# Strassen's products for five token blocks in place of four, with a newly drawn order of steps

## The chip, the cores and the metric

The kernel runs on 1 core of one Trainium2 chip. The metric is the device time of one execution in microseconds (us), median of three runs. Engines are named as the profile names them: PE is TensorE's matmul pipe and PEld its weight loads, DVE is VectorE, ACT is ScalarE, POOL is GpSimd, SP is SyncE, which issues nearly all DMAs.

## The reference

Linear attention over 8 batches and 8 heads, followed by two large products with a gate between them. All data is float32.

```
q_s = softmax(q, axis=-1)            # q, k, v: (8, 8, 576, 64)
k_s = softmax(k, axis=2)
kv  = einsum('bhsd,bhse->bhde', k_s, v)
a   = einsum('bhsd,bhde->bhse', q_s, kv)
x   = a.transpose(0, 2, 1, 3).reshape(4608, 512)
h   = x @ w_in                       # w_in:  (512, 2048)
g   = h * cos(h)
out = g @ w_out                      # w_out: (2048, 512)
```

## The kernel before

The 4608 tokens are nine blocks of 512: block b (0 to 7) holds the first 512 tokens of batch b, block 8 the 64 tokens left over from each batch. The 2048 columns of `h` are 16 slices f of 128. A **unit** u is one block times one slice, 144 in all. Blocks 0 and 1 are done by halves (units 0 to 31 are blocks 0 and 1, slices 0 to 7, then 8 to 15), and from unit 32 each block is 16 units in a row: block 2 is units 32 to 47, block 3 is 48 to 63, block 4 is 64 to 79, block 5 starts at unit 80.

A float32 product is made from three products of split operands (high part, low part): weights `wh`, `wl` against data `xh`, `xl`, without `wl*xl`. An ordinary unit (`unit1`) multiplies 4 chunks of 128 rows of `w_in` by the 128x512 block of x: 4 x 3 = 12 matmuls of 512 columns into one PSUM bank `h` (line 1159). Then the gate runs on ACT and DVE in turn: `turns` (ACT, line 1165), `rest` (DVE, 1169), `cos` (ACT, 1175), `gate` (DVE, 1181), the high part `ghi` (ACT, 1192) and the low part `glo` (DVE, 1198). `unit2` adds the unit's share of the output into four banks `acc` (PE, line 1402, 12 matmuls), two units later.

Blocks from `SB` on go another way for the first product: two slices f, f+1 at a time, `products(u)` uses Strassen's method in Winograd's form on the 2x2 split of x (left and right half of its 512 rows, even and odd tokens): 7 products of 2 x 3 matmuls with 256 columns each (line 1274) in place of 24 matmuls of 512. Product names are T1, B11, B21, T2, T3, B22, T4. T1 and B11 go to a bank `pb`; ACT copies from `pb` into the two `h` banks (`seed`, line 1293) and into `p5` (line 1297), and DVE adds twice (lines 1300 and 1303). The gate and the second product are as before.

Two things have to be there for it:

- Sums and differences of the weights' quarters. `combine(a)` makes those of the slices 2a and 2a+1 (8 calls): 8 DVE steps (lines 1341 to 1364), two ACT casts (1360), and writes to `combined` in DRAM. From there SP loads pieces of 512 KB into the places of `w_in` slices 6 to 13 (`piece`), 28 for a block.
- Sums and differences of the quarters of x (`x_parts`, lines 876 to 907), in place of `x_lo` (line 1025). Their places are those of `w_in` slices 0 to 5.

So `w_in` itself must be out of use by then, and all calls of `combine` lie between unit 32 and the last unit before block `SB`, `2 * (SB - 2)` units apart.

While one block is multiplied, the attention of the next is computed on the same engines: `load_k`, `k_exps`, `kv_rows` and `k_steps` (the kv product on PE, line 710; its normalisation on DVE, lines 690 to 694, 734, 758), `q_steps` (softmax of q, lines 795 to 826), and `x_steps` (q transposed by 32x32 blocks on DVE, line 1047; x on PE, line 989). In units 0 to 23 the weights are also converted from the form in which they come in (`convert`: ACT lines 464 and 469, DVE `shift` 475 and `sign` 486, then the split 498 to 509).

Every step is first added to a `Plan` with its engine. The list `ORDER` of step numbers then sets the order in which all steps are issued; each engine, SP's queue among them, works through its own steps in that order and waits for semaphores where data is not there.

Of the kernel before, what the change touches and what calls it, by code (L numbers as in the profile page):

```python
# [48 lines left out]
    SB=5,  # L49
# [9 lines left out]
7 17 4 0 1 80 81 82 12 2 3 74 75 83 76 160 161 77 78 79 162 163 164 5 6 8 9 10 11 31 13 14 34 35 84 36 44 85 15 16 18  # L59
19 37 45 46 47 92 94 105 28 93 106 38 39 42 20 21 54 48 55 142 143 56 49 40 223 224 225 144 41 43 95 22 23 156 96 57  # L60
58 59 145 146 157 62 24 25 86 87 26 27 50 226 227 97 72 98 52 100 88 29 30 64 51 53 101 107 65 243 244 89 66 90 108
245 311 246 91 60 61 117 109 112 179 180 181 67 99 68 110 102 113 334 63 119 312 313 130 111 319 69 182 120 122 32 33
114 121 125 118 147 165 166 320 203 204 205 70 131 314 123 321 322 323 158 71 73 148 126 127 124 132 167 183 184 185
134 236 237 238 133 137 324 247 149 150 315 316 338 339 317 318 186 135 330 331 325 206 207 159 208 136 138 353 340
139 239 196 197 198 326 327 332 355 341 240 333 173 174 342 151 152 153 209 210 356 357 228 154 155 168 169 170 187
192 335 175 229 358 359 343 347 360 361 188 189 263 264 230 328 115 116 211 193 194 336 337 171 172 329 344 345 362
363 199 346 349 350 351 366 364 352 365 231 190 191 348 354 377 195 176 177 178 103 104 212 213 379 378 380 202 381
216 217 248 278 279 280 281 369 370 382 287 288 200 232 233 201 383 388 222 218 219 220 214 215 783 367 368 371 798
799 265 266 384 302 303 385 389 390 249 250 372 221 373 391 267 268 374 234 269 375 235 251 252 376 392 579 580 464
393 289 394 395 256 257 513 514 304 242 290 140 141 258 259 270 398 400 271 282 241 399 426 283 284 272 253 254 784  # L70
785 528 529 530 515 401 291 285 621 622 292 791 262 403 552 553 404 402 409 293 255 294 295 554 786 792 793 516 128
129 405 406 484 260 794 410 261 273 305 306 274 275 411 412 795 296 297 286 307 603 604 567 568 413 414 451 415 416
452 419 298 299 444 796 531 569 308 517 605 606 797 309 518 789 790 800 420 421 276 277 310 300 301 429 485 445 386
387 465 623 624 625 446 787 788 827 810 811 812 639 640 447 448 422 431 519 532 423 555 520 533 813 814 494 495 626
435 436 437 570 1084 1085 571 428 432 433 434 457 458 474 427 430 459 424 475 675 676 425 441 460 461 815 828 829 830
831 467 468 469 453 677 678 477 801 802 454 449 450 534 438 607 556 641 642 535 557 455 478 479 808 809 396 397 608
470 471 456 462 463 466 487 832 480 481 833 581 582 816 627 472 473 558 559 572 488 489 834 835 803 804 657 658 836
643 476 482 594 595 817 818 483 486 490 491 573 574 583 584 492 493 596 597 497 505 498 499 598 585 496 442 443 918
919 506 507 679 504 508 586 599 500 501 521 819 509 560 600 659 660 661 837 849 850 864 865 601 609 662 522 663 610
510 523 502 503 512 511 536 537 611 612 628 644 805 561 562 524 525 629 1298 1299 806 807 563 820 821 439 440 540 630  # L80
526 527 539 538 543 587 564 541 542 575 576 565 588 589 822 823 680 590 645 591 544 545 549 550 551 613 631 614 681
546 577 646 647 709 710 615 616 566 578 824 592 648 838 602 593 632 633 634 664 665 620 617 1440 1441 618 649 650 635
851 852 636 1129 666 682 683 667 841 842 619 638 637 668 651 652 1130 1131 1138 853 866 867 854 656 653 684 685 920
921 669 670 671 672 693 673 654 655 686 694 687 688 839 840 843 844 674 922 923 547 548 704 705 689 692 690 691 845
700 855 856 1139 703 706 707 708 714 715 695 696 697 724 846 698 699 701 725 726 825 711 712 713 857 868 858 860 719
720 847 702 716 717 718 727 728 407 408 869 861 870 735 736 737 738 739 848 879 880 826 859 731 732 733 881 882 1140
743 744 751 1141 1142 721 734 729 730 742 752 745 746 747 740 741 894 895 722 723 924 925 883 417 418 926 927 871 753
873 1132 872 875 884 885 759 874 750 748 749 758 896 897 932 934 935 754 755 767 756 757 876 886 1133 1134 887 760 761
762 928 929 763 898 930 931 933 947 948 888 890 775 1158 1151 1152 899 891 766 900 892 893 889 901 768 769 776 777 902
764 765 774 1145 903 904 905 770 771 772 906 936 937 1143 909 778 773 779 780 962 910 1135 1136 1137 782 1148 1149  # L90
1150 911 912 1159 1160 1146 1147 1153 1154 781 941 939 963 913 964 965 966 1155 1156 1157 942 943 938 944 945 946 949
877 878 1144 950 951 1016 1017 973 974 957 958 975 976 977 1161 1186 940 1162 1163 1164 1165 1166 981 952 953 989 1167
914 915 982 983 984 954 985 969 970 959 971 967 968 990 1175 1178 1179 1176 1177 1180 1181 972 978 1182 979 960 961
991 992 1183 997 1184 1185 993 1018 980 988 994 1724 1725 1187 1188 995 986 987 1005 998 1006 955 956 999 1000 996
1007 1001 1008 1197 1198 1019 1020 1199 1200 1201 1189 1190 1212 1213 1214 1215 1009 1021 862 863 1202 1203 1168 1169
1002 1003 1170 1022 1023 1026 1027 1028 1030 1031 1191 1192 1035 1036 1037 1004 1010 1011 1043 916 917 1044 1045 1469
1470 1471 1216 1038 1039 1034 1042 1171 1172 1204 1205 1193 1194 1195 1046 1029 1047 1196 1242 1243 1051 1206 1207
1059 1217 1218 1219 1052 1053 1040 1041 1050 1054 1055 1478 1048 1060 1061 1049 1479 1062 1480 1481 1056 1482 1067
1208 1173 1057 1032 1033 1086 1087 1174 1088 1089 1063 1058 1066 1221 1222 1209 1220 1090 1091 1024 1025 1092 1093
1068 1069 1064 1227 1228 1472 1473 1474 1065 1491 1492 1070 1071 1072 1075 1105 1074 1229 1230 1231 1076 1077 1078  # L100
1079 1098 1096 1097 1368 1369 1099 1106 1232 1233 1234 1082 1083 1107 1113 1223 1224 1108 1109 1235 1236 1237 1121
1498 1100 1101 1080 1244 1245 1475 1493 1499 1500 1073 907 908 1114 1488 1489 1490 1210 1211 1104 1246 1247 1081 1112
1238 1239 1248 1249 1250 1122 1094 1095 1494 1495 1123 1124 1125 1110 1111 1120 1115 1116 1117 1118 1485 1486 1487
1119 1251 1253 1252 1254 1257 1496 1497 1370 1371 1280 1258 1126 1259 1260 1102 1103 1302 1127 1261 1128 1267 1303
1304 1291 1262 1264 1483 1484 1476 1477 1501 1526 1281 1292 1282 1283 1293 1284 1294 1265 1268 1269 1270 1321 1502
1503 1504 1505 1225 1226 1506 1295 1515 1516 1517 1507 1271 1508 1509 1263 1322 1323 1324 1325 1266 1305 1306 1510
1272 1273 1274 1329 1307 1277 1287 1288 1289 1290 1285 1286 1330 1296 1511 1331 1332 1518 1519 1278 1279 1529 1530
1527 1528 1520 1521 1522 1337 1297 1333 1338 1339 1320 1328 1340 1275 1276 1308 1310 1311 1345 1523 1524 1341 1353
1525 1537 1538 1334 1531 1326 1335 1327 1300 1301 1346 1354 1347 1348 1355 1309 1552 1553 1240 1241 1532 1349 1356
1314 1357 1336 1344 1539 1540 1541 1361 1342 1343 1352 1533 1512 1542 1543 1544 1362 1363 1364 1365 1312 1313 1546  # L110
1315 1391 1350 1351 1534 1554 1555 1360 1392 1393 1394 1513 1535 1536 1514 1012 1013 1654 1655 1395 1366 1545 1556
1557 1358 1367 1399 1407 1316 1317 1786 1547 1558 1559 1787 1788 1359 1548 1390 1398 1795 1796 1797 1400 1408 1401
1402 1403 1415 1549 1409 1410 1411 1396 1397 1318 1319 1372 1561 1562 1373 1404 1798 1582 1583 1567 1568 1569 1570
1571 1789 1405 1790 1791 1808 1799 1809 1810 1584 1585 1560 1572 1563 1423 1374 1565 1566 1564 1375 1416 1417 1418
1419 1424 1425 1406 1414 1376 1377 1378 1379 1382 1383 1426 1431 1427 1255 1256 1811 1812 1813 1384 1386 1387 1385
1388 1389 1461 1802 1792 1573 1815 1412 1413 1420 1421 1803 1804 1574 1575 1586 1576 1577 1578 1579 1814 1805 1800
# [135 lines left out]
def linear_attention_then_cos_gated_mlp(  # L252
# [85 lines left out]
    q_rows = dr.tile([2, S, P], F32, name="q_rows")  # L338
    SB = CFG["SB"]
    NOP = 7 * NF // 2  # L340
# [583 lines left out]
    def x_steps(b, p, place, kvw, tq, tx, due_q, due_x, xr=None):  # L924
# [147 lines left out]
        us = 0.6 if whole else 0.37  # L1072
        if b >= SB:
            e = floats(b, p)
# [581 lines left out]
```

## Time and profile before

| | |
|---|---|
| median of three runs | 832.1 us (831.51 to 832.5) |
| the profiled execution | 831.63 us, of which the span from first to last instruction is 829.8 us |
| granted TensorE clock over the span | 1.000 |
| matmuls recorded | 4884: 960 on line 1159 (units 0 to 79), 1344 on line 1274 (units 80 to 143, 32 pairs x 42), 1656 on line 1402, and those of the attention |
| start of unit 80 (first matmul of line 1274) | 491.5 us after the span's start |

Of an engine's row the busy time is the union of its instructions. A matmul's end is modelled and reaches over the start of the next one, so what a matmul costs in a row of matmuls is read from the distance of their starts, or from a piece of the chain of work divided by its count.

### The profile page before, as it was taken

The numbers are of one execution on the slowest core, as the hardware profiler recorded it, in microseconds if no ns is written. First come the engines' busy times: TensorE is split into PE (matmuls) and PEld (weight loads), VectorE is DVE, ScalarE is ACT, GpSimd is POOL, SyncE is SP. The second block draws the span as 40 slices with busy tenths as digits, with TensorE's granted clock in tenths as the row PEclk, the third lists the DMA queues.
The fourth block names the chain that finished last, engine by engine and source line by source line (L and its number), as shares of the span: only waits on it lengthen the run. The fifth ranks groups of instructions, "written<-read, shape, count | busy, mean of one in ns | idle before, by whom it ended". The sixth has DMA issues, their size and how long they took to land.

```text
span 829.8 us, 13645 instructions
## 1 busy us (share of the span) xinstructions
PE 801.2 (97%) x4884; PEld 705.1 (85%) x4884; DVE 639.1 (77%) x1084; ACT 532.0 (64%) x958; POOL 41.6 (5%) x161
## 2 busy tenths in 40 slices
PE   2899999999999999999999999999999999999997
PEld 1666788788888888888888898999999999999996
DVE  7999999988768976888788878788877645664443
ACT  4999998655456557664764667677756546555441
POOL 1100100000100110002000110002000000000000
PEclk9999999999999999999999999999999999999999
DMA  8888182324635651563535886998788587665521
GB/s 252 258 221 310 55 273 69 106 70 119 181 83 138 176 161 45 150 183 100 152 107 146 219 254 220 252 268 261 208 234 246 198 287 238 224 199 189 188 106 51
DMA packets 196036, 149.28 MB, mean 180 GB/s; under 512 B 110464, under 2 KB 172416, under 8 KB 195968
## 3 DMA queue, kind: packets, MB, share of 16 engines
q1 hardware_dynamic: 195648, 147.89, 59.7%
q8 instruction: 38, 0.62, 0.3%
q10 hardware_dynamic: 320, 0.52, 0.2%
q14 instruction: 30, 0.25, 0.1%
HBM read 114.03 MB, written 34.34 MB: 179 GB/s over the span
## 4 chain that ended last, share of the span: by engine, by line
PE 78%; DVE 5%; ACT 4%; DMA 1%; issue 1%; SPq 1%; ACTq 0%
PE acc L1402 38%; PE h L1159 19%; PE h L1274 13%; PE pb L1274 5%; PE x_False L989 2%; PE kv L710 1%; DVE kt L1181 1%; DMA raw_o<-in_moe_w_out_dram 1%; DMA w_io<-combined 1%; DVE w_o L509 1%; ACT L1175 0%; DVE glo L1198 0%; DVE kt L1169 0%; ACT kt L1175 0%; ACT raw_io L464 0%
## 5 line engine op out<-in xcount | busy, mean ns | idle before, releaser
L1402 PE MATMUL acc<-w_o,ghi 128*128 128x512 f32 x552 | 164.5, 380 | 0.0
L1159 PE MATMUL h<-x,w_i 128*128 128x512 f32 x660 | 152.5, 383 | 2.2 <-DVE kt L1181 2.0
L1165 ACT ACTIVATE kt<-h 128x512 int32<-128x512 f32 x144 | 86.1, 600 | 106.6 <-PE h L1274 57.3
L1159 PEld LDWEIGHTS h<-x,w_i 128*128 128x128 f32 x660 | 123.5, 189 | 22.1 <-DVE kt L1181 4.1
L1169 DVE SCALAR_TENSOR_TENSOR kt<-kt,h 128x512 f32<-128x512 int32 x144 | 97.9, 684 | 41.9 <-ACT kt L1165 41.1
L1181 DVE TENSOR_TENSOR kt<-kt,h 128x512 f32<-128x512 f32 x138 | 93.6, 686 | 34.5 <-ACT kt L1175 32.7
L1175 ACT ACTIVATE kt<-kt 128x512 f32<-128x512 f32 x144 | 90.3, 633 | 46.0 <-DVE kt L1169 45.3
L1402 PEld LDWEIGHTS acc<-w_o,ghi 128*128 128x128 f32 x552 | 101.3, 189 | 12.8 <-DVE o L1449 0.2
L1402 PE MATMUL acc<-w_o,glo 128*128 128x512 f32 x276 | 105.0, 381 | 0.2 <-DVE glo L1198 0.2
L1402 PE MATMUL acc<-w_io,ghi 128*128 128x512 f32 x296 | 88.4, 380 | 0.0
L1192 ACT CAST ghi<-kt 128x512 fp32r<-128x512 f32 x106 | 64.5, 618 | 26.0 <-DVE kt L1181 18.1
L1198 DVE TENSOR_TENSOR glo<-kt,ghi 128x512 fp32r<-128x512 f32 x106 | 71.7, 685 | 11.0 <-ACT ghi L1192 10.6
L1402 PE MATMUL acc<-w_o,w_io 128*128 128x512 f32 x288 | 72.9, 379 | 0.0
L1159 PE MATMUL h<-x,w_io 128*128 128x512 f32 x300 | 68.0, 379 | 1.1 <-DVE kt L1181 1.1
L1159 PEld LDWEIGHTS h<-x,w_io 128*128 128x128 f32 x300 | 56.0, 189 | 9.1 <-DVE kt L1181 1.5
L1402 PEld LDWEIGHTS acc<-w_o,glo 128*128 128x128 f32 x276 | 52.2, 189 | 9.0 <-DVE glo L1198 1.8
L1402 PEld LDWEIGHTS acc<-w_io,ghi 128*128 128x128 f32 x296 | 53.8, 189 | 6.6
L1402 PEld LDWEIGHTS acc<-w_o,w_io 128*128 128x128 f32 x288 | 51.6, 190 | 5.7
L1402 PE MATMUL acc<-w_io,glo 128*128 128x512 f32 x148 | 56.1, 379 | 0.0
L1274 PE MATMUL h<-x,w_i 128*128 128x256 f32 x320 | 48.3, 275 | 0.0
L1274 PEld LDWEIGHTS h<-x,w_i 128*128 128x128 f32 x320 | 44.6, 191 | 1.7 <-ACT h L1293 0.2
L1274 PE MATMUL h<-w_i,w_i 128*128 128x256 f32 x280 | 44.6, 276 | 0.8 <-ACT h L1293 0.7
(155 smaller groups left out, 1321.4 us busy)
## 6 DMA issues: line engine op xcount, KB each, us to landing
w_i<-combined SPq DMA_DIRECT2D x70, 512.0 KB, 4.8
w_io<-combined SPq DMA_DIRECT2D x42, 512.0 KB, 5.0
out_dram<-o SPq DMA_DIRECT2D x32, 256.0 KB, 2.5
k<-in_k_dram SPq DMA_DIRECT2D x14, 512.0 KB, 4.3
q<-in_q_dram SPq DMA_DIRECT2D x28, 256.0 KB, 3.5
qb<-q_rows SPq DMA_DIRECT2D x96, 72.0 KB, 2.6
q_rows<-q SPq DMA_DIRECT2D x24, 256.0 KB, 2.5
raw_i<-in_moe_w_in_dram SPq DMA_DIRECT2D x11, 512.0 KB, 5.4
```

What stands on the lines that cost most here:

```text
L509: nc.vector.tensor_sub(split(l), dealt(c), split(h))
L710: nc.tensor.matmul(x[h * D : (h + 1) * D, odd : odd + vt.shape[1]], t[:, h, c, :], vt, start=(c == CM), stop=(c == CM - 1),)
L989: nc.tensor.matmul(t[:, 0:HALF], a, c[:, cs] if whole else woven(c[:, cs]), start=(n == 0), stop=(n == len(parts) - 1 and not again))
L1159: nc.tensor.matmul(o, a, woven(x), start=(c == 0 and n == 0), stop=(c == KC - 1 and n == 2))
L1165: nc.scalar.activation(t, T["h", u], AF.Identity, bias=0.25, scale=1.0 / TWO_PI)
L1169: nc.vector.scalar_tensor_tensor(t.bitcast(F32), t, -TWO_PI, T["h", u], op0=ALU.mult, op1=ALU.add)
L1175: nc.scalar.activation(t, t, AF.Sin, bias=0.5 * math.pi)
L1181: nc.vector.tensor_mul(o, t, T["h", u])
L1192: nc.scalar.copy(t, T["kt", u].bitcast(F32))
L1198: nc.vector.tensor_sub(t, T["kt", u].bitcast(F32), T["gh", u].bitcast(F32))
L1274: nc.tensor.matmul(dst(), w[:, cs], x.rearrange("p a i -> p i a"), start=start and j == 0 and n == 0, stop=j == 1 and n == 2, skip_group_c ...
L1402: nc.tensor.matmul(T["acc", j], a[:, js], woven(w), start=(first and n == 0), stop=(last and n == 2))
```

## The change

`SB` goes from 5 to 4: block 4 (units 64 to 79) is done by Strassen's products too. Its 192 matmuls of line 1159 go, 8 pairs of 42 on line 1274 come. The eight calls of `combine` now come every 4 units from unit 32 to 60, in place of every 6 from 32 to 74. `x_parts` runs for block 4 as well. The choice of due times `att2`/`att3` also shifts by one block with `SB`, but due times don't enter the program: the order does. `ORDER` is another list from its first numbers on (3769 steps in place of 3575). Lines behind the list stand 8 further down in the kernel of after.

```
-    SB=5,
+    SB=4,
...
 ORDER = """
-7 17 4 0 1 80 81 82 12 2 3 74 75 83 76 160 161 77 78 79 162 163 164 5 6 8 9 10 11 31 13 14 34 35 84 36 44 85 15 16 18
...
```

Three places show how the list moves instructions.

The first is DVE in unit 18 (block 0, slice 10), where the names carry the unit: `kt_18`, `h_18`, `glo_16`; `raw_io13` is the raw weight slice 13 in conversion, `kvw_2_2` and `kvt_2_2` belong to the attention of block 2, head pair 2. Before:

```order
L734 SCALAR_TENSOR_TENSOR kvt_2_2_1594<-kv_2_2_1487,r_2_2_1590,mask_83 128x128
L507 TENSOR_TENSOR w_io12_1581<-wc_io12_1571,w_io12_1581 128x512
L509 TENSOR_TENSOR w_io12_1581<-wc_io12_1571,w_io12_1581 128x512
L1198 TENSOR_TENSOR glo_16_1603<-kt_16_1534,ghi_16_1601 128x512
L1181 TENSOR_TENSOR kt_17_1576<-kt_17_1576,h_17_1509 128x512
L1169 SCALAR_TENSOR_TENSOR kt_18_1638<-kt_18_1638,h_18_1613 128x512
L758 TENSOR_TENSOR kvw_2_2_1641<-kvt_2_2_1594,kvw_2_2_1641 128x128
L475 SCALAR_TENSOR_TENSOR raw_io13_1150<-raw_io13_1150 128x1024
L1181 TENSOR_TENSOR kt_18_1638<-kt_18_1638,h_18_1613 128x512
L475 SCALAR_TENSOR_TENSOR raw_io15_1210<-raw_io15_1210 128x1024
```

The same place of the changed kernel, around the same `gate` of unit 18 (line 1189 there):

```order
L1189 TENSOR_TENSOR kt_17_1554<-kt_17_1554,h_17_1539 128x512
L1055 STREAM_TRANSPOSE qf_2_0_1604<-qb_2_0_1590 128x576
L1177 SCALAR_TENSOR_TENSOR kt_18_1620<-kt_18_1620,h_18_1606 128x512
L515 TENSOR_TENSOR w_io12_1601<-wc_io12_1563,w_io12_1601 128x512
L517 TENSOR_TENSOR w_io12_1601<-wc_io12_1563,w_io12_1601 128x512
L1189 TENSOR_TENSOR kt_18_1620<-kt_18_1620,h_18_1606 128x512
L483 SCALAR_TENSOR_TENSOR raw_io13_1059<-raw_io13_1059 128x1024
L494 SCALAR_TENSOR_TENSOR wc_io13_1639<-raw_io13_1059 128x1024
L1177 SCALAR_TENSOR_TENSOR kt_19_1675<-kt_19_1675,h_19_1649 128x512
L1206 TENSOR_TENSOR glo_17_1696<-kt_17_1554,ghi_17_1633 128x512
```

The `shift` of slice 13 now stands behind the gate, and so does that of slice 14, and six steps of block 2's kv (`kvw_2_1`, `kvt_2_2`, `kvw_2_2` and the three short ones of `r_2_2`); the transpose `qf_2_0` has come in ahead. The other DVE steps ahead of this gate are the same in both kernels.

The second is PE where the Strassen blocks begin: unit 80 before, unit 64 after (`pb_80`, `h_80`; `h_80` holds unit 80, `w_i7` is the place of a loaded piece). Before:

```order
L1274 MATMUL pb_80_5062<-x_5_0_4745,w_i6_857 128x256 x3
L1274 MATMUL pb_80_5062<-x_5_1_4931,w_i6_857 128x256 x3
L1402 MATMUL acc_64_0_4321<-w_io13_1689,ghi_77_5052 128x512 x2
L1402 MATMUL acc_64_0_4321<-w_io13_1689,glo_77_5054 128x512
L1402 MATMUL acc_64_1_4365<-w_io13_1689,ghi_77_5052 128x512 x2
L1402 MATMUL acc_64_1_4365<-w_io13_1689,glo_77_5054 128x512
L1402 MATMUL acc_64_2_4371<-w_io13_1689,ghi_77_5052 128x512 x2
L1402 MATMUL acc_64_2_4371<-w_io13_1689,glo_77_5054 128x512
L1402 MATMUL acc_64_3_4375<-w_io13_1689,ghi_77_5052 128x512 x2
L1402 MATMUL acc_64_3_4375<-w_io13_1689,glo_77_5054 128x512
L1274 MATMUL h_80_5091<-x_5_2_4806,w_i7_975 128x256 x3
L1274 MATMUL h_80_5091<-x_5_3_4988,w_i7_975 128x256 x3
```

After (line 1282 is 1274 of before):

```order
L1282 MATMUL pb_64_4247<-x_4_0_3973,w_i6_888 128x256 x3
L1282 MATMUL pb_64_4247<-x_4_1_4137,w_i6_888 128x256 x3
L1282 MATMUL h_65_4267<-w_i2_560,w_i7_1013 128x256
L1282 MATMUL h_65_4267<-w_i0_325,w_i7_1013 128x256
L1282 MATMUL h_65_4267<-w_i2_560,w_i7_1013 128x256 x2
L1282 MATMUL h_65_4267<-w_i1_521,w_i7_1013 128x256
L1282 MATMUL h_65_4267<-w_i2_560,w_i7_1013 128x256
L1282 MATMUL h_64_4284<-x_4_2_3994,w_i7_1013 128x256 x3
L1282 MATMUL h_64_4284<-x_4_3_4176,w_i7_1013 128x256 x3
L1282 MATMUL pb_66_4292<-x_4_0_3973,w_i9_1374 128x256
```

Before, 12 matmuls of unit 77's second product stand between B11 and the first product that needs a seed; after, T2 follows B11 at once.

The third is DVE at the end of block 3 (units 62 and 63, attention of block 4 in `x_4_...`, `xf_4_1`). Before:

```order
L1025 TENSOR_TENSOR x_4_3_4107<-x0_4_3_False_4072,x_4_3_4107 128x288
L1025 TENSOR_TENSOR x_4_3_4107<-x1_4_3_False_4076,x_4_3_4107 128x224
L1169 SCALAR_TENSOR_TENSOR kt_63_4102<-kt_63_4102,h_63_3972 128x512
L1356 TENSOR_TENSOR sum_5_4041<-sum_5_4041 128x256
L1364 TENSOR_TENSOR sum_5_4041<-sum_5_4041,sumhi_5_0_4119 128x512
L1181 TENSOR_TENSOR kt_62_4098<-kt_62_4098,h_62_3946 128x512
```

After:

```order
L893 TENSOR_TENSOR x_4_3_4176<-xf_4_1_4115,x_4_3_4176 128x512
L897 TENSOR_TENSOR xf_4_1_4115<-xf_4_1_4115 128x2x128
L1177 SCALAR_TENSOR_TENSOR kt_63_4112<-kt_63_4112,h_63_4041 128x512
L897 TENSOR_TENSOR xf_4_1_4115<-xf_4_1_4115 128x2x128 x3
L1189 TENSOR_TENSOR kt_62_4105<-kt_62_4105,h_62_4028 128x512
L913 TENSOR_TENSOR w_i1_521<-xf_4_1_4115,x_4_1_4137 128x2x2x128
L915 TENSOR_TENSOR w_i1_521<-xf_4_1_4115,w_i2_560 128x512
L1189 TENSOR_TENSOR kt_63_4112<-kt_63_4112,h_63_4041 128x512
```

Where two `x_lo` (line 1025) and `combine`'s sixth call (`sum_5`) stood, the steps of `x_parts` for head pairs 1 and 3 now stand between the last gates of block 3; the last call of `combine` (`sum_7`) lies some 40 rows further ahead.

One more place is told in words alone, as its rows read alike: ahead of unit 6's first product PE had the second products of units 0 to 3 before, and has those of units 0 to 2 after; ahead of the gate that this product waits for (unit 4's), DVE has three conversion steps of 512 columns fewer and one `x_lo` more. In front of unit 20's first product PE has three matmuls of a second product fewer than before.

## Rows read from the trace of the kernel before

**Rows 1.** The page: busy time by engine, and PE's busy tenths in 40 slices.

```profile
PE 801.2 (97%) x4884; PEld 705.1 (85%) x4884; DVE 639.1 (77%) x1084; ACT 532.0 (64%) x958; POOL 41.6 (5%) x161
...
PE   2899999999999999999999999999999999999997
```

**Rows 2.** By stretch: us, busy (x) of PE, PEld, DVE, ACT, POOL; clock, DMA share, GB/s.

```profile
40.00:160.00 120.00, 115.74 (x615) 88.05 (x616) 114.68 (x173) 108.63 (x173) 6.45 (x11) 1.00 0.53 169
160.00:225.70 65.70, 65.70 (x316) 57.92 (x315) 54.45 (x88) 36.53 (x66) 3.90 (x23) 1.00 0.48 130
225.70:405.60 179.90, 179.84 (x1058) 157.86 (x1057) 142.85 (x237) 109.17 (x177) 12.85 (x54) 1.00 0.47 129
405.60:491.50 85.90, 85.90 (x477) 75.53 (x477) 71.02 (x119) 53.47 (x93) 5.77 (x26) 1.00 0.64 183
491.50:658.90 167.40, 166.61 (x1184) 155.42 (x1182) 133.89 (x230) 113.02 (x222) 5.54 (x26) 1.00 0.81 237
```

**Rows 3.** Who PE waited for over the whole span: us, times, longest.

```profile
PE h L1159 <- DVE kt L1181: 3.1, 3, 1.3
PE h L1274 <- ACT h L1293: 0.7, 1, 0.7
```

**Rows 4.** The chain that ended last, from 120 to 160 us: start, us, what.

```profile
149.10 0.17 DVE r L691
...
154.51 1.46 DVE raw_io L475
155.97 0.64 DVE kt L1181
...
156.65 2.86 PE h L1159 x12
```

**Rows 5.** The same chain later: two of its pieces on PE.

```profile
165.98 5.18 PE h L1159 x24
...
495.69 1.34 PE h L1274 x12
```

**Rows 6.** Groups by line and shape, DVE: xcount, then busy us, mean ns, idle before.

```profile
L1047 DVE STREAM_TRANSPOSE qf<-qb 128x576 f32<-128x576 f32 x24 | 18.5, 771 | 2.3 <-DMA qb<-q_rows 2.3
...
L889 DVE TENSOR_TENSOR xf<-xf 128x256 f32<-128x256 f32 x32 | 13.6, 425 | 0.5
...
L475 DVE SCALAR_TENSOR_TENSOR raw_io<-raw_io 128x1024 int32<-128x1024 int32 x5 | 7.5, 1528 | 0.0
...
L734 DVE SCALAR_TENSOR_TENSOR kvt<-kv,r,mask 128x128 f32<-128x128 f32 x24 | 8.4, 350 | 0.6
...
L1341 DVE TENSOR_TENSOR sum<-w_i 128x512 f32<-128x512 f32 x11 | 7.5, 703 | 0.0
...
L1025 DVE TENSOR_TENSOR x<-x_False,x 128x288 fp32r<-128x288 f32 x16 | 7.2, 452 | 3.2 <-ACT x L1003 3.2
L758 DVE TENSOR_TENSOR kvw<-kvt,kvw 128x128 fp32r<-128x128 f32 x24 | 6.9, 286 | 2.0 <-ACT kvw L754 2.0
```

**Rows 7.** Groups by line and shape, ACT.

```profile
L1293 ACT COPY h<-pb 128x256 f32<-128x256 f32 x64 | 22.8, 362 | 14.5 <-DVE kt L1181 12.2 <-PE pb L1274 1.7
```

**Rows 8.** PE in order of time at the wait on line 1293: start, us, what, idle before.

```profile
515.00 0.94 PE L1274 MATMUL h<-w_i,w_i 128*128 128x256 f32 x6 [0.73 <-ACT h L1293]
```

**Rows 9.** By stretches of 20 us, columns as in rows 2.

```profile
100.00:120.00 20.00, 18.41 (x83) 15.09 (x82) 19.10 (x29) 19.31 (x28) 1.75 (x2) 1.00 0.66 202
120.00:140.00 20.00, 19.25 (x119) 16.11 (x119) 19.31 (x27) 19.43 (x25) 0.00 (x0) 1.00 0.29 102
140.00:160.00 20.00, 18.90 (x94) 15.29 (x91) 18.40 (x27) 13.47 (x23) 0.31 (x1) 1.00 0.26 93
160.00:180.00 20.00, 20.00 (x94) 17.53 (x93) 18.37 (x28) 11.90 (x20) 0.00 (x0) 1.00 0.52 125
```

**Rows 10.** DMA issues: xcount, KB each, median us from issue to landing.

```profile
w_i<-combined SPq DMA_DIRECT2D x70, 512.0 KB, 4.8
```

**Rows 11.** Groups by line and shape, PE: the second product of units 0 to 5.

```profile
L1395 PE MATMUL acc<-room,g 128*128 128x512 f32 x48 | 22.0, 595 | 0.2 <-DVE g L1181 0.2
```

## What the change will do: the prediction

> **What bounds the kernel now.** I read the page first, then busy times by stretch, then the waits and the chain. On the page PE is busy 97% of the span, and only its first slices show room [rows 1]. The stretches say where that room is [rows 2]. From 40 to 160 us PE is idle 4.3 of 120 us, while DVE is busy 114.7 of 120 (96%): in these units the weights are still being converted, and DVE sets the pace. From 160 to 659 us PE is idle 0.06 + 0.79 = 0.85 us in all, while DVE is busy 83, 79, 83 and 80%: here PE's own work is the bound. The waits [rows 3] name DVE's gate (line 1181) for 3.1 us, the largest after PE has got going, and ACT's seed (line 1293) for 0.7. The chain shows the place where the one regime ends [rows 4]: shift of a weight slice 154.51, gate 155.97, then PE's 12 matmuls of unit 20 at 156.65; behind it pieces of PE follow one another [rows 5]. So what the change takes off PE's work behind 160 us counts in full, and so does whatever moves the point 156.65.
>
> **Change, term 1: PE's work.** 24 matmuls of 512 columns take 5.18 us, 0.2158 each; 12 of 256 columns take 1.34, 0.1117 each [rows 5]. Block 4 loses 16 x 12 = 192 of the first, 192 x 0.2158 = 41.4 us, and gets 8 x 42 = 336 of the second, 336 x 0.1117 = 37.5 us. That is -3.9 us. The loss-free limit would be 336 x 0.2158 / 2 = 36.3, so the narrow matmuls' extra cost is already in.
>
> The Trainium skill speaks against this term: in "TensorE: Matmul & The Clock Gate", section "Back-to-back issue gap", the spacing in a real kernel is set by weight load and matmul together, about 131 ns at 512 columns and 81 at 128. 256 lies one doubling from either, so an estimate is their mean, 106 ns, and by that the change would lose 336 x 0.106 - 192 x 0.131 = 10.5 us. The trace has 216 and 112 ns at a load per matmul, so the measurement decides; it fits the same section's formula for a single gap, N/2.4 + 2.5 ns.
>
> **Term 2: the start.** The list is new from its first number, and the place to look at is the gate of unit 18, which unit 20's product waits for. In the shown order two shifts of 1.528 us, two `kvw` of 0.286, one `kvt` of 0.350 and three steps of about 0.17 have gone behind it, 4.5 us; a transpose of 0.771 has come ahead [rows 4, 6]. DVE, always busy there, reaches the gate 3.7 us earlier. PE has three matmuls less done by then (0.65), so unit 20 gains 3.0 us at most. Against it stands unit 6, where PE has one second product less done, 22.0 / 6 = 3.7 us [rows 11], and DVE three conversion steps less (half of 1.528 each, 2.3) and one `x_lo` more (0.45): PE is 1.8 us worse there. But PE lost 1.59 + 0.75 + 1.10 = 3.4 us between 100 and 160 [rows 9], that is behind unit 6, so a wait that is 1.8 longer at unit 6 leaves 3.4 - 1.8 = 1.6 us of gain at least, if no third place is late. Range 0 (another place takes it all) to -3.0; I take -2.4, the middle of 1.6 and 3.0 rounded up, as waits too short to be shown as idle go as well.
>
> **Term 3: the entry into block 4.** PE runs T2 directly behind B11 in the new order. T2 needs the seed: 0.362 us on ACT [rows 7] and two hand-overs. The one such wait in the trace is 0.73 us [rows 8]. I take +0.7. A second one lurks: `x_parts` of head pairs 1 and 3 must be ready before the first product. Behind the last x matmul PE has two second products and the kv product, 2 x 2.59 + 2.5 = 7.7 us, as cover; the chain on DVE alone is one step of 0.7, four of 0.425, two of 0.7, with a `rest` and a gate of 0.69 between, 5.2 us [rows 6], and about four ACT steps of 0.4 to 0.6 in series, 2. It just fits: 0 to 1 us, with 0.3 taken in term 4.
>
> **Term 4: DVE in blocks 2 and 3.** One `combine` is four steps of 512 columns (0.70) and four of 256 (0.42): 4.5 us [rows 6]. Eight calls in units 32 to 63 in place of 5 1/3 add 12.0. `x_parts` is 6 x 0.70 + 10 x 0.425 = 8.5 us and replaces eight `x_lo` of at most 0.452 (3.6): 4.9 more. Together 142.9 + 16.9 = 159.8 us in the 180 us from 225.7 to 405.6, 89% in place of 79% [rows 2]. At 96% PE waited, at 83% it didn't, and the 20 us behind 160 show 92% with PE at 20.00 of 20 [rows 9]. So 89% should mostly fit. Bounds: 0, or, if no more than 83% were to be had without waits, 159.8 / 0.83 - 180 = 12.5 us. I take the near end with +0.8, for one or two waits of about 0.5 and the 0.3 of above.
>
> **What I cost at nothing.** In block 4 the seeds, the copies to `p5` and the adds are 8 x (2 x 0.362 + 0.38) = 8.8 us more on ACT and 8 x 2 x 0.43 = 6.9 on DVE, but ACT is busy 62% there and DVE loses two calls of `combine` that now lie earlier (9 us) [rows 2]. DMA: 28 pieces of 512 KB more, each 4.8 us to landing [rows 10]. Block 5 of before has the same pieces beside the attention of the next block, and that whole stretch runs at 81% of DMA time with 0.79 us of PE idle [rows 2]; cover gone, each late piece costs up to 4.8 us.
>
> **Sum.** The profiled execution took 831.63 us. 831.63 - 3.9 - 2.4 + 0.7 + 0.8 = 826.8. The median of the runs is 832.1, 0.5 above it: **827.3 us**, 0.6% faster.
>
> **Rivals.**
> A, the forecast: all four terms about as above, 824.6 to 829.3. Chance 0.62.
> B, the start gives nothing: some place other than unit 20 in the new list is as late. Its ground is that DVE's total work up to unit 20 is nearly the same and 1.8 us worse at unit 6. 827.3 + 2.4 = 829.7. Chance 0.15, two thirds of it still faster by over 0.2%.
> C, the other side: DVE becomes the bound in blocks 2 and 3, gates come late and PE waits unit after unit. Place: units 32 to 63, above all block 3, where `x_parts` and four calls of `combine` meet. Price up to 12.5 us: 827.3 - 0.8 + 12.5 = 839.0. It outweighs the gain (4.8 + 0.8 = 5.6 us) when DVE can't be held above 159.8 / 185.6 = 86% without waits. The 92% row speaks against, the 96% row with its waits for it. Chance 0.12, of which 0.07 slower.
> D, pieces from `combined` come late in block 4, since the writes of the last calls and the loads of the first pieces now fall nearer together: one piece late by a whole landing, 827.3 + 4.8 = 832.1, no change. Two would be slower. Chance 0.08.
> E, narrow matmuls cost more than their share of columns: from 192 / 336 x 0.2158 = 0.123 us each the change loses. The rows have 0.1117 over 1344 of them. Chance 0.01. By the spacing that the Trainium skill gives ("TensorE: Matmul & The Clock Gate", "Back-to-back issue gap") the time would be 827.3 + 3.9 + 10.5 = 841.7, an estimate.
> The rest, 0.02, is a slower start.
>
> 0.2% (1.7 us) is about what a measurement of this kernel can tell from no change. Faster by more, below 830.4: A, 0.10 of B, 0.02 of C, 0.02 of D: 0.76. Same: 0.05 of B, 0.03 of C, 0.04 of D: 0.12. Slower: 0.12. The range that leaves out 2 in 10 goes from the full gain at the start with no new waits, 832.1 - 3.9 - 3.0 = 825.2, less 0.5 for short waits that go, to B with one more wait of a microsecond: 824.7 to 830.8.
>
> **What would show it.** Term 1: 768 matmuls on the ordinary line, 1680 on the Strassen line, at 0.216 and 0.112 us; block 4 some 4 us shorter. Term 2: the point from which PE pieces follow unbroken lies 1.6 to 3 us before 156.65, and DVE's gate no longer stands before unit 20. Term 3: one wait of about 0.7 us for line 1301 (the old 1293) at unit 65. Term 4: DVE near 89% in blocks 2 and 3, and PE idle under 1 us there. The forecast is wrong if PE shows rows of waits for `glo` or gates in units 32 to 63, if DMA releases the Strassen products, or if PE at unit 20 is no earlier.

## The result, and the profile after

The changed kernel takes **824.5 us** (median of four executions, 823.86 to 826.6) where the kernel before takes 832.3 beside it (831.51 to 833.34): ratio 0.991, 95% interval 0.989 to 0.993. In a later round of runs it was 824.9 against 831.0, ratio 0.9924 (0.9907 to 0.9941). It is faster, as forecast, by 6 to 8 us in place of the forecast 4.8; the first median lies 0.2 us below the low end of the range (824.7). The profiled execution took 826.60 us, of which the span is 824.8.

The page, to be read against [rows 1]: busy time by engine, then PE in 40 slices.

```profile
PE 798.3 (97%) x5028; PEld 708.5 (86%) x5028; DVE 648.2 (79%) x1108; ACT 531.6 (64%) x982; POOL 46.1 (6%) x161
...
PE   2899999999999999999999999999999999999997
```

Busy time by stretch of the kernel after, the same stretches as [rows 2], then those of [rows 9]: length, PE, PEld, DVE, ACT, POOL; clock, DMA share, GB/s.

```profile
40.00:160.00 120.00, 118.13 (x602) 92.30 (x601) 115.52 (x171) 110.13 (x180) 8.30 (x12) 1.00 0.63 194
160.00:225.70 65.70, 65.70 (x317) 57.95 (x316) 57.82 (x94) 37.79 (x67) 5.26 (x24) 1.00 0.47 132
225.70:405.60 179.90, 179.45 (x1067) 158.01 (x1066) 153.33 (x264) 108.23 (x185) 10.90 (x54) 1.00 0.60 169
405.60:491.50 85.90, 85.90 (x589) 80.29 (x590) 70.18 (x119) 61.45 (x117) 5.50 (x26) 1.00 0.85 247
491.50:658.90 167.40, 165.73 (x1230) 154.19 (x1229) 132.49 (x229) 108.80 (x218) 6.25 (x26) 1.00 0.82 245
...
100.00:120.00 20.00, 19.64 (x92) 16.91 (x91) 19.32 (x27) 17.68 (x27) 3.76 (x2) 1.00 0.56 183
120.00:140.00 20.00, 20.00 (x128) 17.37 (x127) 19.70 (x28) 17.17 (x22) 0.31 (x1) 1.00 0.59 162
140.00:160.00 20.00, 20.00 (x94) 17.43 (x93) 19.90 (x26) 17.03 (x26) 0.00 (x0) 1.00 0.36 121
```

From 40 to 160 us PE's idle time falls from 4.3 to 1.9 us while DVE is as busy as before (115.5 against 114.7): the same work stands in a better order. Between 120 and 160 PE is not idle at all, where it had lost 0.75 and 1.10 [rows 9]. In 225.7 to 405.6 DVE has 10.5 us more to do and PE hardly notices (0.45 us idle, and that is the entry into block 4 at 404). In 491.5 to 658.9 PE is idle 1.7 us, more than before; 1.5 of it is one wait, below.

The waits of PE, whole span (us, times, longest), against [rows 3]:

```profile
PE h L1282 <- ACT h L1301: 1.9, 2, 1.5
...
PE h L1167 <- DVE kt L1189: 0.4, 1, 0.4
```

The gate, 3.1 us before, is down to 0.4. The seed (line 1301, the old 1293) has two waits in place of one. The chain of work shows where DVE now hands over to PE for the last time ahead of 160 us, against [rows 4, 5] ("issue" is time in which nothing that is shown was waited for):

```profile
108.90 0.70 DVE kt L1189
109.60 0.04 issue
109.64 2.86 PE h L1167 x12
112.50 4.53 PE acc L1410 x21
117.03 5.18 PE h L1167 x24
...
485.40 1.34 PE h L1282 x12
```

This is unit 12's product. From 109.64 us on the chain is pieces of PE alone to behind 160, where before it went back to DVE up to unit 20 at 156.65. The pieces have their old price, 5.18 / 24 = 0.216 and 1.34 / 12 = 0.112 us a matmul.

The two waits for the seed, in order of time. First the entry into block 4, in the chain:

```profile
402.10 1.55 PE pb L1282 x12
403.65 0.02 issue
403.67 0.37 ACT h L1301
404.04 0.04 issue
404.08 1.60 PE h L1282 x12
```

PE marks it as 0.45 us idle. It is a new wait. The one of the kernel before [rows 8], at 515.0 us, did not stand at its entry (unit 80, 491.5 us) but at unit 84. There 21 matmuls of second products stood between B11 and T2, and the seed was late for another reason: ahead of it on ACT stood a copy of the output (line 1452) that had waited for an output transfer:

```profile
514.08 0.59 ACT L1452 COPY o<-acc 128x512 f32<-128x512 f32 x1 [0.89 <-DMA out_dram<-o]
514.56 0.38 ACT L1293 COPY h<-pb 128x256 f32<-128x256 f32 x1
```

In the kernel after, unit 84 has no wait, and unit 80 has none in either kernel. The second wait for the seed, in the timeline of all engines after:

```profile
632.12 0.78 DVE L1055 STREAM_TRANSPOSE qf<-qb 128x576 f32<-128x576 f32 x1 [2.37 <-DMA qb<-q_rows]
632.83 0.65 DVE L1189 TENSOR_TENSOR kt<-kt,h 128x512 f32<-128x512 f32 x1
...
633.51 0.36 ACT L1301 COPY h<-pb 128x256 f32<-128x256 f32 x1 [2.47 <-DVE kt L1189]
...
633.92 0.94 PE L1282 MATMUL h<-w_i,w_io 128*128 128x256 f32 x6 [1.48 <-ACT h L1301]
```

Read from the top: a transpose waits 2.37 us for q's rows from DRAM; a gate is queued behind it on DVE; the seed needs the accumulator that this gate frees; PE needs the seed. One late transfer, three engines on, is 1.5 us of PE.

### The profile page after: what moved, and what is told of

Its sections match the earlier page's. It is cut to its first block, busy times and chain, and to the rows that moved or that the text cites. A ratio compares the mean times of both kernels' runs of the same rounds, so it can differ in the third digit from the quotient of the medians.

```text
span 824.8 us, 14005 instructions
## 1 busy us (share of the span) xinstructions
PE 798.3 (97%) x5028; PEld 708.5 (86%) x5028; DVE 648.2 (79%) x1108; ACT 531.6 (64%) x982; POOL 46.1 (6%) x161
## 4 chain that ended last, share of the span: by engine, by line
PE 88%; DMA 4%; ACT 3%; SPq 2%; DVE 1%; issue 1%; POOL 0%; POOLq 0%; DVEq 0%; ACTq 0%
PE acc L1410 41%; PE h L1167 18%; PE h L1282 16%; PE pb L1282 6%; PE x_False L997 3%; PE acc L1403 2%; PE kv L718 2%; DMA raw_o<-in_moe_w_out_dram 2%; DMA raw_i<-in_moe_w_in_dram 1%; DMA q_rows<-q 1%; DMA qb<-q_rows 0%; ACT kt L1183 0%; SPq L621 0%; SPq L617 0%; SPq L553 0%
## 5 line engine op out<-in xcount | busy, mean ns | idle before, releaser
L1410 PE MATMUL acc<-w_o,ghi 128*128 128x512 f32 x504 | 150.0, 379 | 0.0
L1167 PE MATMUL h<-x,w_i 128*128 128x512 f32 x528 | 121.8, 383 | 0.5 <-DVE kt L1189 0.4
L1167 PEld LDWEIGHTS h<-x,w_i 128*128 128x128 f32 x528 | 98.9, 189 | 16.7 <-issue 1.2
L1410 PE MATMUL acc<-w_o,glo 128*128 128x512 f32 x252 | 95.6, 379 | 0.0
L1410 PE MATMUL acc<-w_o,w_io 128*128 128x512 f32 x360 | 90.9, 380 | 0.0
L1410 PEld LDWEIGHTS acc<-w_o,w_io 128*128 128x128 f32 x360 | 64.9, 190 | 7.2
L1282 PE MATMUL h<-x,w_i 128*128 128x256 f32 x410 | 61.9, 276 | 0.2 <-DVE h L1308 0.2
L1282 PEld LDWEIGHTS h<-x,w_i 128*128 128x128 f32 x410 | 56.9, 192 | 2.5 <-DVE h L1308 0.4
L1282 PE MATMUL h<-w_i,w_i 128*128 128x256 f32 x358 | 57.1, 276 | 0.4 <-ACT h L1301 0.4
L1167 PE MATMUL h<-x,w_io 128*128 128x512 f32 x240 | 54.3, 379 | 0.0
L1282 PEld LDWEIGHTS h<-w_i,w_i 128*128 128x128 f32 x358 | 49.5, 192 | 2.2 <-ACT h L1301 0.9
```

Of the source, the lines that this page charges most:

```text
L1167: nc.tensor.matmul(o, a, woven(x), start=(c == 0 and n == 0), stop=(c == KC - 1 and n == 2))
L1282: nc.tensor.matmul(dst(), w[:, cs], x.rearrange("p a i -> p i a"), start=start and j == 0 and n == 0, stop=j == 1 and n == 2, skip_group_c ...
L1410: nc.tensor.matmul(T["acc", j], a[:, js], woven(w), start=(first and n == 0), stop=(last and n == 2))
```

## The experiments

All times are medians, each beside the kernel before in the same round. The kernel before moved between 831.0 and 832.0 us over these rounds, so ratios are compared.

| run | us | before | ratio (95%) |
|---|---|---|---|
| e1_start | 831.3 | 831.0 | 0.9995 (0.9985 to 1.0004) |
| e2_block4 | 840.5 | 831.0 | 1.0105 (1.0090 to 1.0121) |
| e3_after_again | 824.9 | 831.0 | 0.9924 (0.9907 to 0.9941) |
| e4_transpose_later | 824.8 | 831.0 | 0.9919 (0.9906 to 0.9932) |
| e5_start_blocks01 | 828.2 | 831.6 | 0.9954 (0.9936 to 0.9972) |
| e6_blocks2on | 828.7 | 831.6 | 0.9959 (0.9944 to 0.9974) |
| e7_load_ahead_of_18 | 828.3 | 831.6 | 0.9958 (0.9943 to 0.9974) |
| e8_dve_blocks23 | 839.4 | 831.6 | 1.0084 (1.0069 to 1.0100) |
| e9_dve_half | 830.0 | 832.0 | 0.9980 (0.9970 to 0.9990) |
| e10_dve_quarter | 826.7 | 832.0 | 0.9934 (0.9921 to 0.9946) |
| e11_old_units0to5 | 826.0 | 832.0 | 0.9925 (0.9912 to 0.9937) |
| e12_dma_more | 838.5 | 832.0 | 1.0074 (1.0060 to 1.0087) |

**The parts apart: start against block 4.** The theory is that the start and block 4 each bring their own share and add up; the rival, B, is that the start brings nothing. Two lists were spliced: one list up to a unit's first product, the other behind it. In e1 it is the kernel before, with the head of the new list:

```diff
     SB=5,
 ...
 ORDER = """
-7 17 4 0 1 80 81 82 12 2 3 74 75 83 76 160 161 77 78 79 162 163 164 5 6 8 9 10 11 31 13 14 34 35 84 36 44 85 15 16 18
+17 4 7 31 12 28 0 1 80 81 82 2 3 74 75 76 5 6 83 84 8 9 42 77 78 79 92 94 93 10 11 13 14 34 35 36 44 37 45 38 46 39 40
...
```

> The kernel before (SB = 5, block 4 by plain products), with the steps up to unit 24's first product in the order that the changed list has, the rest in the old order. If the start is a gain of its own (term 2, and what the trace after shows: PE loses 3.1 us less ahead of 160 us and begins 0.3 earlier), the time is 832.3 - 3.4 = 828.9 us, and PE's waits between 100 and 160 us fall from about 3.4 us to under 1. If the new start gives nothing (rival B) and the whole gain comes from block 4 and from what stands behind 160 us, it is 832.3 within 0.5.

Measured: no change, as the rival has it. But the trace shows the start's gain and then two places that take it back. Unit 20 begins at 152.35 us, as in the kernel after, not at 156.65. PE then lost 1.5 us around 183, at the splice, and 2.0 around 464, where this row of the timeline stands:

```profile
465.05 1.00 PE L989 MATMUL x_False<-qt,kvw 128*128 128x288 f32 x6 [0.93 <-ACT xf L1011]
```

Ahead of it the four loads of q's rows kept SP's queue for 3.51 us in place of 2.05. Why they did is not settled. The splice itself is at fault as much as the theory, so this run decides nothing alone.

The reverse, e2: the kernel after with the old list's head, cut at the same unit.

```diff
     SB=4,
 ...
 ORDER = """
-17 4 7 31 12 28 0 1 80 81 82 2 3 74 75 76 5 6 83 84 8 9 42 77 78 79 92 94 93 10 11 13 14 34 35 36 44 37 45 38 46 39 40
+7 17 4 0 1 80 81 82 12 2 3 74 75 83 76 160 161 77 78 79 162 163 164 5 6 8 9 10 11 31 13 14 34 35 84 36 44 85 15 16 18
...
```

> The kernel after (SB = 4, block 4 by Strassen's products), with the steps up to unit 24's first product in the old order, the rest as the new list has it. If the two parts add up (terms 1 and 3 here, term 2 in the other run), it is slower than the kernel after by the 3.1 to 3.4 us of the start: 824.5 + 3.3 = 827.8 us, or 832.3 - 3.9 + 0.9 = 829.3 by the terms. If block 4 alone brought the whole gain (rival B), it is 824.5 within 0.7. If the Strassen products of block 4 were worth nothing, 832.3.

Measured: 9.5 us slower than before, which no theory had. The waits of PE in this run have a row that neither kernel has:

```profile
PE x_False L997 <- DVE qt L985: 8.3, 1, 8.3
```

The stretches at its end show a second price (columns as above, the clock third from the right):

```profile
188.00:190.00 2.00, 0.00 (x0) 0.00 (x0) 2.00 (x3) 0.22 (x1) 0.00 (x0) 0.50 0.00 0
190.00:192.00 2.00, 1.59 (x5) 1.42 (x6) 1.90 (x4) 1.01 (x2) 0.00 (x0) 0.50 0.00 0
...
194.00:196.00 2.00, 2.00 (x6) 1.60 (x5) 0.00 (x0) 0.01 (x1) 0.00 (x0) 0.50 0.00 0
```

At the splice q's input is asked for late and DVE waits for it; PE stands for 8.3 us, the granted clock falls to 0.50 (1.2 GHz), and it is still there from 194 to 196, with PE at work again since 190.4. The run says nothing on the change. Both splices were made again at unit 32, the end of blocks 0 and 1. e5 is e1 with the later cut:

> The kernel before (SB = 5), with all steps up to unit 32's first product (blocks 0 and 1) in the new order and the rest in the old. The splice of the first such run stood at unit 24, where PE waited 1.5 us at 183 us, and 2.0 us more went at 464 us, so that nothing of the 3.8 us that the start had gained was left. If the start's gain counts in full where the splice stands well (term 2), PE loses some 3.5 us less ahead of 160 us, nothing at the splice, and the time is 831.0 - 3.4 = 827.6 us. If blocks 2 to 4 in the old order take back whatever the start gains (the wait at 464 us in the first run), it is 829.5 to 831.5.

Measured: 0.9954, 3.4 us off the 831.6 beside it. Unit 32 begins at 222.32 us (225.74 before, 222.38 after), PE idles nowhere new, and the wait at 464 is gone. e6 is e2 with the later cut:

> The kernel after (SB = 4), with all steps up to unit 32's first product in the old order and the rest in the new. The first such run, cut at unit 24, had a wait of 8.3 us at 182 us that neither kernel has: q's rows were asked for late at the splice. If the parts add up (terms 1, 3, 4 here, term 2 in the start), the time is that of the kernel after plus the start: 824.9 + 3.4 = 828.3 us. If Strassen's products in block 4 and the new order behind unit 32 brought everything, 824.9. If they brought nothing, 831.0.

Measured: 0.9959, 2.9 us off. The two parts sum to 0.0087 of the time; the whole change took 0.0076 and 0.0090 of it in its two rounds. So the change is two gains of about 3 us each, and rival B falls. e6 takes in the Strassen products of block 4 and the new order behind unit 32 together; no run tells these two apart, and the products' own price is read from counts and distances (term 1, below).

**What sets the start.** In the kernel after, the last subtraction of units 12 to 16 is done twice, which leaves every value as it is:

```diff
         def lo():
...
-            nc.vector.tensor_sub(t, T["kt", u].bitcast(F32), T["gh", u].bitcast(F32))
+            for _ in range(2 if 12 <= u < 17 else 1):
+                nc.vector.tensor_sub(t, T["kt", u].bitcast(F32), T["gh", u].bitcast(F32))
```

> The kernel after, with the subtraction at line 1206 done twice (the same result) in units 12 to 16: five steps of 0.686, 3.4 us more work on DVE ahead of unit 18's gate. By term 2 it is the work that DVE has ahead of that gate which sets when unit 20 starts, and unit 20 sets all that follows: the time goes up by what the start had gained, 3.0 to 3.4 us, to 828.1, and PE's waits between 100 and 160 us come back. If the start's end is set elsewhere (the loads, ACT, unit 6), the time stays within 0.7 us of 824.9.

Measured: 828.3, ratio 0.9958 against 0.9924, 2.8 us. The chain again goes through DVE to unit 20's product:

```profile
157.07 0.61 DVE kt L1189
157.68 0.04 issue
157.72 2.86 PE h L1167 x12
```

This profiled execution took 830.1 us, 1.9 above its median, and was already 1.9 late at unit 4 (59.75 against 57.87 us), so the 5.0 us by which unit 20 is later than in the kernel after (152.70) are 3 of DVE's and 2 of that. The gate of unit 18 is the place, as term 2 had it.

The other half of term 2 was the 1.8 us by which PE was to be worse at unit 6. e11 puts the old order back up to unit 6's first product (367 steps) and keeps the new one behind it.

> The kernel after, with the steps up to unit 6's first product in the old order and the rest in the new. The prediction had PE 1.8 us worse at unit 6 by the new order, and PE does lose some 1.2 us more between 40 and 60 us in the trace after. If unit 20 (DVE's work ahead of unit 18's gate) sets the end of the start, as by term 2, what is won at unit 6 is waited out behind it: the same within 0.5 us, 824.9. If unit 6 sets it now, 1 to 1.8 us faster, 823.4, and a better version than either kernel.

Measured: 0.9925 against 0.9924, the same. Unit 7 begins at 88.61 us in this run, at 88.43 and 88.65 in the two profiles of the kernel after, whatever stands ahead of it. Against the second profile of the kernel after, PE idles 0.80 us less from 40 to 60 us, and 1.51 more from 60 to 100. So unit 6 has no price of its own; I had taken a place that is late for the one that sets the time.

**How much DVE would stand in blocks 2 and 3.** Rival C, by the same doubled subtraction, in all units of 32 to 63 (e8, shown), in every second (e9, `u % 2`) and in every fourth (e10, `u % 4 == 1`):

```diff
-            nc.vector.tensor_sub(t, T["kt", u].bitcast(F32), T["gh", u].bitcast(F32))
+            for _ in range(2 if 32 <= u < 64 else 1):
+                nc.vector.tensor_sub(t, T["kt", u].bitcast(F32), T["gh", u].bitcast(F32))
```

> The kernel after, with the subtraction at line 1206 done twice in units 32 to 63: 32 x 0.686 = 22 us more work on DVE in blocks 2 and 3, where it is busy 85.2% of 180 us: 97.4% if PE were not held up. It prices rival C, that DVE becomes the bound there. If DVE can be filled to 92% without PE waiting (as in the 20 us behind 160 of the kernel before), (153.3 + 22.0) / 0.92 - 180 = 10.5 us are lost, 835.4. If no more than 86% were to be had (the point at which rival C would decide), 175.3 / 0.86 - 180 = 23.8 us, 848.7. If all of it is hidden, 824.9.

> The kernel after, with the subtraction at line 1206 done twice in every second unit of 32 to 63: 16 x 0.686 = 11.0 us more on DVE in blocks 2 and 3, half of the last such run, in which 22 us more cost 14.5 and DVE stood at 173.0 of 192.8 us, 89.7%. If DVE has a ceiling of 89.7% there (a late form of rival C), (153.7 + 11.0) / 0.897 = 183.6 us for blocks 2 and 3 in place of 179.65: 3.9 us more, 828.8. If the cost is in proportion (14.5 / 22 a microsecond from the first one on), 7.2 more, 832.1. If half of it is hidden between PE's work and nothing waits, 824.9.

> The kernel after, with the same subtraction done twice in every fourth unit of 32 to 63: 8 x 0.686 = 5.5 us more on DVE, which makes 159.2 us, the load that term 4 had estimated for blocks 2 and 3 (159.8, 89%; the trace after has 153.7, 85.6%). It shows what that load would have cost. With a ceiling of 89.7%: 159.2 / 0.897 = 177.5, under the 179.65 there are, so nothing, 824.9 within 0.7. In proportion (0.66 for each microsecond): 3.6 more, 828.5. By term 4's own figure: 0.8 more, 825.7.

Busy time from the first product of unit 32 to that of unit 64, columns as above, first in the kernel after:

```profile
222.38:402.03 179.65, 179.65 (x1058) 158.00 (x1056) 153.73 (x261) 107.68 (x182) 13.01 (x64) 1.00 0.61 171
```

The same two units in e10, with 5.5 us more on DVE:

```profile
222.38:403.03 180.65, 180.14 (x1058) 157.58 (x1056) 158.63 (x269) 106.95 (x181) 13.25 (x64) 1.00 0.61 170
```

In e9, with 11.0 us more:

```profile
221.84:406.11 184.27, 182.07 (x1058) 157.07 (x1056) 162.83 (x276) 107.13 (x181) 13.06 (x64) 1.00 0.60 167
```

In e8, with 22.0 us more:

```profile
221.93:414.75 192.82, 183.41 (x1058) 157.09 (x1056) 172.73 (x291) 107.05 (x181) 13.29 (x64) 1.00 0.57 160
```

The stretch grows by 1.0, 4.6 and 13.2 us, and over its whole length DVE stands at 85.6, 87.8, 88.4 and 89.6%. The first 5.5 us of extra work are mostly hidden; of the last 11.0, nearly each microsecond counts ((13.2 - 4.6) / 11.0 = 0.8). The medians, by ratio to e3, say 0.8, 4.7 and 13.3. e9 is near the branch with a ceiling (4.6 measured, 3.9 expected), and e10 cost 1.0 where a sharp ceiling had nothing and term 4's own figure 0.8.

But DVE's share over the whole stretch is not what sets the loss, as its parts show. In e10 0.8 of the 1.0 us go between units 48 and 54, at one gate (0.51 us of PE idle). Over these units DVE is busy 84% of the time, but just ahead of that gate it works without a pause; its steps of `combine` and of the attention stand there together with three `glo`, one of them the added one:

```profile
315.71:342.99 27.28, 26.77 (x192) 23.12 (x191) 22.86 (x37) 19.05 (x30) 1.39 (x2) 1.00 0.63 195
326.00:332.00 6.00, 5.50 (x26) 4.48 (x24) 5.86 (x13) 2.89 (x6) 0.00 (x0) 1.00 0.70 191
```

In e9 over half of the 4.6 us goes at the same units, and behind them DVE is busy 94% of 60 us while PE is idle for 0.34 us:

```profile
345.50:406.11 60.61, 60.27 (x356) 52.03 (x354) 56.87 (x99) 36.55 (x66) 5.60 (x26) 1.00 0.75 207
```

So extra work costs time where it makes a gate late, and these runs price it at the units where they put it; a ceiling on DVE's share is not shown.

**The wait at 632.** The kernel after once more:

> The kernel after, unchanged, for a second profile and a closer interval. In the first profile (826.6 us, the slowest of four executions) PE waits 1.48 us at 633.9 for a seed on ACT, behind a gate that stood behind a transpose which waited 2.37 us for its rows from q_rows. If that wait is a matter of this one execution, it is missing here or under 0.5 us, and the profiled execution is at 824 to 825. If the order makes it, it is here again at 1 us or more.

Measured: the profiled execution took 825.16 us, and the wait is not there. The transpose starts when its turn comes, with nothing idle ahead of it:

```profile
629.29 0.69 DVE L1189 TENSOR_TENSOR kt<-kt,h 128x512 f32<-128x512 f32 x1
629.89 0.77 DVE L1055 STREAM_TRANSPOSE qf<-qb 128x576 f32<-128x576 f32 x1
630.59 0.65 DVE L1189 TENSOR_TENSOR kt<-kt,h 128x512 f32<-128x512 f32 x1
```

e4 moves the transpose (step 3023) and the rounding of the same rows (3024) down the list:

```diff
-3006 2841 2842 3019 3020 2829 2837 2838 3021 3022 3023 2823 2845 2824 3009 2847 3010 2957 3024 2958 2793 2828 2796
-2825 3011 3012 3013 3014 2827 3015 2848 2846 2850 3025 2881 2875 2876 2882 3034 3035 2839 2840 2851 2853 3017 2852
+3006 2841 2842 3019 3020 2829 2837 2838 3021 3022 2823 2845 2824 3009 2847 3010 3023 2957 2958 2793 2828 2796 2825
+3024 3011 3012 3013 3014 2827 3015 2848 2846 2850 3025 2881 2875 2876 2882 3034 3035 2839 2840 2851 2853 3017 2852
```

> The kernel after with one transpose of q's rows (block 7, second quarter, the one that waited 2.37 us at 632) moved seven steps down the list, behind unit 107's gate and the next split of x, and the rounding of the same rows three steps down. If the list's order makes the wait in every execution, PE's wait near 634 goes and the time falls by 1 to 1.5 us, to 823.2. If the wait was an accident of the profiled execution, the time is that of the kernel after within 0.4 us.

Measured: the same time as e3. The wait is one of single executions (of the other traces with this order only e10's has it, 2.04 us before the transpose), not of the list. It accounts for 1.5 of the 2 us by which the first profile is above its median, and for nothing of the change.

**Transfers in block 4 (rival D).**

```diff
-                nc.sync.dma_start(
-                    T[piece(n)].bitcast(F32).rearrange("p n (h c) -> p n h c", h=2), combined[:, 2 * m : 2 * m + 2]
-                )
+                for _ in range(2 if u < 80 and n % 4 == 0 else 1):
+                    nc.sync.dma_start(
+                        T[piece(n)].bitcast(F32).rearrange("p n (h c) -> p n h c", h=2), combined[:, 2 * m : 2 * m + 2]
+                    )
```

> The kernel after, with every fourth of the 28 pieces of block 4 loaded twice from combined (the same data): 7 x 512 KB more, where the DMA engines are busy 87% of the 80 us and move 20.4 MB. It prices rival D, that pieces come late in block 4. At the rate of this stretch, 20.4 MB in 69.5 us of busy time, 3.7 MB are 12.5 us, and 10.4 us are free. If any free DMA time serves, 2.1 us are left over, 827.0. If each doubled piece comes late by a part of its 4.9 us to landing (SP's queue is in order, and q's rows stand behind the pieces), it is 7 x 1 to 7 x 4.9 = 7 to 34 us, 832 to 859. If there is room for all of it, 824.9.

Measured: 838.5, ratio 1.0074 against 0.9924, 12.5 us. That lies in the range of the second branch (832 to 859), and by its cause: what stands behind the doubled pieces in SP's queue comes late. SP waited from 395 to 500 us in a way that the kernel after doesn't have:

```profile
SPq L1251 <- DMA w_i<-combined: 26.6, 6, 6.2
```

SP holds the second load of a piece until the first has landed, and all that is queued behind it. So the run prices 26.6 us of a blocked queue and not 3.7 MB, and what more bytes alone would cost stays open. It does show two chains by which a blocked queue comes through to PE, and the change itself has neither:

```profile
PE h L1283 <- DMA w_i<-combined: 5.1, 1, 5.1
PE acc L1411 <- ACT o L1461: 3.4, 1, 3.4
```

The first is a late piece. The second is a copy of the output on ACT that had waited 5.86 us for an output transfer, issued by the same queue. Behind each of the two waits the granted clock was lower for some microseconds (0.75 from 428 to 432 us, 0.56 from 464 to 468). The waits are 8.5 of the 12.5 us; matmuls that followed each other at a wider distance there are some 3.8.

## Why the prediction was right, and where its terms were off

The sign and the two sources were right, the gain too small: 4.8 us forecast, 6.1 and 7.8 measured. Against the second profile (825.16 - 831.63 = -6.5 us), by the prediction's own steps:

**Term 1, PE's work: -3.9, measured -3.9.** Both line counts are as forecast (768 and 1680), at 0.216 and 0.112 us. Counted at these distances, the two lines together go from 357.3 to 353.4 us; this is counts times distances, no run has the products alone. Rival E falls by the 0.112. By an estimate, the spacing that the Trainium skill gives ("TensorE: Matmul & The Clock Gate", "Back-to-back issue gap"), 131 ns at 512 columns and 81 at 128, would have made the change a loss; the trace of the kernel after doesn't agree, with 216 ns at 512 columns and 112 at 256. Block 4 alone, unit 64 to unit 80, went from 85.9 to 79.9 us, 6.0 and not 4; second products that now cross its ends are in that, so such marks price no term.

**Term 2, the start: -2.4, measured -3.1 to -3.4.** Unit 32 begins 3.4 us earlier in the first profile and in e5, 3.1 in the second (222.66). The mechanism was right (e5, e7), and the gate of unit 18 starts 4.0 us earlier (155.91 before, 151.89 after) where 3.7 were forecast. DVE was not "always busy there", though: ahead of that gate it had waited 1.24 us for ACT (`turns` of unit 18). The size was off at the step "a wait that is 1.8 longer at unit 6 leaves 3.4 - 1.8 = 1.6 us of gain at least": e11 shows that unit 6 takes nothing. The place that sets the end now is unit 12, at 109.64 us, and it is no later than it was (109.55). So all that PE lost behind unit 12 is won, a little more than the upper end of 3.0, and that end was the value to take.

**Term 3, the entry into block 4: +0.7, measured +0.45 to +0.61, and taken back at a place that no term had.** The wait is there, at the place forecast and nearly of the size (0.45 idle, 0.61 from start to start beyond the usual distance). But the step that took its price from [rows 8] was a misreading. That wait had nothing to do with T2 directly behind B11: it stood at unit 84, behind a copy of the output that had waited for a transfer. That the two sizes are near each other is luck. And that wait is gone with the new order: 0.73 us in the kernel before, 0.42 and 0.52 in e1 and e5, which have the old order there, none in the kernel after and in e6. So PE idles 0.79 us from 400 to 570 us before and 0.45 after, and start to start it loses the same in both within 0.1 us. What the entry costs and what unit 84 gives back cancel, which was not forecast. The second wait, for `x_parts`, did not come: its last DVE step ends at 401.0, the first product starts at 402.0.

**Term 4, DVE in blocks 2 and 3: +0.8, measured 0.** PE idles nowhere in 222.38 to 402.03. The load was over-estimated: +16.9 us, 89%, where the trace has +10.9 (142.79 to 153.73, unit 32 to unit 64), 85.6%. Two reasons. Two calls of `combine` more lie in the stretch, not 2 2/3 (14 whole sums of line 1349 where line 1341 had 10 before; a call has two). And the durations that I summed overlap: the durations of all DVE instructions in this stretch sum to 153.5 us before and 167.6 after, 14.0 more, where the busy time grows by 10.9. The price for such a load was about right: e10 put DVE at nearly that load, 158.6 us, with other work at other places, and lost 0.8 to 1.0. The step from a share to a wait was weak all the same, for the forecast and for rival C. e9 has 94% over 60 us with PE idle for 0.34 us, more than the 92% that I held possible, and e10 loses 0.51 us at a gate in 27 us with 84%, as DVE is full just ahead of it. Rival C did not come; e9, with 9.1 us more of DVE's busy time, lost 4.6 us, nearly the gain that was forecast.

**At nothing:** block 4's transfers hold. DMA is busy 85% in 405.6 to 491.5, and PE waits for no piece. ACT and the adds cost nothing there either. Left over in the second profile are some 0.5 us that PE loses more between 570 and 655.

Against the second profile the three small terms erred to the same side, 0.7 + 0.7 + 0.8 = 2.2 us. Less the 0.5 left over that is 1.7, by which 6.5 is more than the forecast 4.8. The 0.7 of term 3 in it is luck: the wait came, and the one at unit 84 went.

No run beat the kernel after. e4 and e11 are equal to it.

## What to carry to other kernels

A wait in a trace is the price of another wait only if both have the same cause: before it is put into a sum, look where it stands and what its releaser had itself waited for. Where one engine sets the pace of a phase, the gain is bounded by the last place that stays late, so look for the place which the change leaves as it was, here unit 12, and not for each place that becomes worse. Room on an engine can't be read from its busy share of a long stage: the same harmless extra work in three doses shows how much is hidden, and the starts of the units show at which place the rest is lost.

## Not expected of the hardware and the profile

DVE's busy share over tens of microseconds told little about whether PE would wait: PE was never idle in 40 us with DVE at 98 to 100% (120 to 160 us of the kernel after), nearly never in 60 us with 94% (e9), and idle for 0.51 us at one gate in 27 us with 84% (e10), where DVE's work was crowded into the microseconds ahead of that gate. Summed durations of DVE exceed its busy time by 9% (167.6 against 153.7 us), since in this trace an instruction starts before the recorded end of the one ahead (632.83 against 632.12 + 0.78 above). And q's rows, in pieces of 72 KB, took 3.4 us to landing (median from 620 to 640 us) in one execution and 2.8 in another of the same program; together with an issue that came 1.2 us later (626.4 against 625.2) that was enough for 1.5 us of PE three engines further on.
